# Second attention accumulator summed on VectorE, first scores in slots of their own, half-width bank last, and one gate/up tile moved from the filler to the seven-product stage

## The chip, the cores and the metric

One core of a Trainium2 chip runs the whole program. Its engines are TensorE (PE in the profile, with its weight loads as PEld), VectorE (DVE), ScalarE (ACT), GpSimd (POOL) and SyncE (SP), which here issues DMAs. Each engine works through its own instructions in order and waits on semaphores for the others. The metric is the device time of one execution in microseconds, taken as the median of several runs. The kernel before has a median of 1060.9 us in 3 runs (1057.14 to 1061.3).

## The reference

One transformer block with a parallel sum: attention and a gated MLP both read the same normalised input, and both results are added to x.

```python
xn  = layernorm(x)                                   # 2048 tokens x 640
q, k, v = split(xn @ wqkv)                           # 32 heads of 20
p   = softmax(mask(q @ k.T / sqrt(20)))              # query i sees keys i-255 .. i
att = (p @ v) @ wo
mlp = (gelu_tanh(xn @ w_gate) * (xn @ w_up)) @ w_down   # inner width 1728
out = x + att + mlp
```

All of it is float32; the mask is a sliding window of 256 keys.

## The kernel before, in words

**Products in three passes.** A float32 product is computed as three products of split operands (high x high, low x high, high x low), each of five 128-row steps, so one 128x512 result of `xn @ w` is 15 matmuls (`dense_steps`, L105 in the profile). Where two gate/up results are wanted for two token chunks at once, `gate_up_pair` (matmuls at L935) computes them with seven block products in place of eight: 54 matmuls for each pair of chunks, 108 for a gate/up tile over all 2048 tokens, where the plain way takes 120.

**Stages.** (1) Layer norm, transposes and the first q/k and v projections, up to about 92 us. (2) Attention, in 32 units, about 92 to 627 us. A unit is 4 heads by one chunk of 512 queries. (3) The pairs: the half tile `rest[0]` plain and then gate/up tiles 6 to 12 by `gate_up_pair`, to about 812 us. (4) The down and output projections, also by seven products (L1202), to the end.

**A unit of attention.** It has 14 slots (`NS`). Each slot emits a few instructions of attention and then pulls matmuls from a generator, `filler()`, at a mean of `RATE / NS` a slot: the remaining q/k/v projections and gate/up tiles 0 to 5. The list `sets` says in which order the filler takes them. Before slot 0 of the first unit a ramp pulls some 112 filler matmuls. The instructions of PE, ACT, DVE and POOL are emitted in exactly this order; SP's order is set by a scheduler.

- *Maxima.* `max_pair` makes two 128x320 score tiles on PE (`ps_m`, L480) in four PSUM buffers, and DVE reduces each to row maxima (`junk`, `mx`, L490). A unit has eight pairs: two at the head of slot 0, two after the values, two each in slots 5 and 9. They run ahead of the unit that needs them.
- *Scores.* `exp_piece` makes one of 12 score pieces on PE (`ps_e`, L545) and ACT exponentiates it (L547) into a probability tile `P`. Four pieces (one for each head) fill one bank; a unit has three banks, called X, Z and Y in `pieces`, in three `P` buffers. Z is half as wide in the first chunk. `ps_e` has two PSUM buffers, tag `ex`.
- *Clearing.* One slot after a bank's fourth piece, `clear` zeroes the masked corners on POOL (L558, L561), 128x512 elements each.
- *Values.* In slot 0 of the next unit `av_unit` multiplies the banks with v (`ps_o`, L586) into two accumulators `os[0]` and `os[1]`, one for each half of the keys' rows. They take the two `ex` buffers, so the next unit's first score piece needs `os[0]` read out, and the second needs `os[1]` read out. ACT copies `os[0]` to `ob` (L592) and `os[1]` to a spare part of Y's `P` tile (L593); three slots later POOL adds the two (L596), and five slots later SP stores `ob`.

**Loads.** `load_stack` brings the stacked q and k tiles of unit u+3 (`qs`, `ks`, six DMAs each): k in slot 9 (`KSLOT`), q in slot 12. Their buffers are free when the score pieces that read the old tiles are done.

**Deferred work.** `defer(n, ...)` runs a step n slots later, `late` puts it behind the slot's attention instructions.

Of the kernel before, what the change touches and what calls it, by code (L numbers as in the profile page):

```python
# [19 lines left out]
C = 512  # L20
# [10 lines left out]
NS = 14  # L31
RATE = 42.2
V1_SLOT = 158
MXD = 7
KSLOT = 9
LAG = 3, 5, 4, 4, 4, 4, 3, 3, 4, 3, 2, 1, 1, 1
NFA = 6
HD = D // 2
# [27 lines left out]
def block_kernel(ctx, tc, x, wqk, wv, wgu, wdo, wdl, out):  # L66
# [464 lines left out]
    def exp_piece(u, s):  # L531
# [15 lines left out]
        nc.scalar.activation(pt[:, j, lo:hi], ps[:, lo:hi], AF.Exp, scale=SCALE)  # L547
        if j == 3:
            defer(1, clear, u, bi)

    def clear(u, bi):
        c = u % NC
        pt = pts[u, bi]
        for p in pieces(c)[bi]:
            for col, diag in diag_tail(*p, c):
                a = pt[:, :, col:col + 128]
                if diag:
                    nc.gpsimd.affine_select(out=a, in_=a, pattern=[[0, 4], [1, 128]], compare_op=OP.is_ge,  # L558
                                            fill=0.0, base=0, channel_multiplier=-1)
                else:  # L560
                    nc.gpsimd.affine_select(out=a, in_=a, pattern=[[0, 4], [-1, 128]], compare_op=OP.is_ge,  # L561
                                            fill=0.0, base=-1, channel_multiplier=1)

    def av_unit(u):
# [5 lines left out]
        def half(d, r):  # L570
            i = 2 * d + r
            return d, r, max(0, 64 * i), min(C, 64 * i + 320)

        steps_ = [((0, 0), (0, 1)), ((2, 0), (-1, 1)), ((-1, 0), (2, 1)), ((1, 0), (1, 1)),
                  ((3, 0), (-2, 1)), ((-2, 0), (3, 1))]
        todo = [half(*x) for pair in steps_ for x in pair if x[0] in place]
        begun_, left = set(), [sum(t[1] == r for t in todo) for r in range(2)]
        for d, r, qa, qb in todo:
# [10 lines left out]
            begun_.add(r)  # L589
        ob, oc = ap.tile([128, C], F32, name="ob", tag="ob", bufs=1), pts[u, 2][:, 0]  # L590
        lo = 0 if c else 64
        nc.scalar.activation(ob, os[0], AF.Copy)  # L592
        nc.scalar.activation(oc[:, lo:], os[1][:, lo:], AF.Copy)  # L593

        def join():
            nc.gpsimd.tensor_tensor(out=ob[:, lo:], in0=ob[:, lo:], in1=oc[:, lo:], op=OP.add)  # L596

# [4 lines left out]

        defer(3, join)
        defer(5, store)

# [183 lines left out]
    def attention():  # L789
# [696 lines left out]
```

## Time and profile before

| what | value |
|---|---|
| median of 3 runs | 1060.9 us |
| the profiled execution's own time | 1059.57 us |
| its span | 1057.7 us |
| PE busy | 1042.1 us (99%) |
| DVE, ACT, POOL busy | 722.2, 532.1, 376.0 us |
| granted TensorE clock | 0.998 on average |
| attention, `ps_o` first to last | 106.1 to 627.1 us |
| pairs, `ps_g` | 627.6 to 812.8 us |

Busy times on PE are modelled ends of pipelined matmuls: a 128x512 matmul is shown as about 0.39 us long although the next one starts about 0.23 us after it. So "99% busy" hides short waits, and they are read from starts, from weight loads that were held up, and from who released them. DMA traffic (44.7% of the DMA engines' span on SP's queue) is not what sets the pace in attention.

### The profile page before, as it was taken

To read this page: it belongs to the slowest core of one execution; us is meant where nothing else is said; L and a number is where in the kernel's file an instruction comes from. 1 tells how busy PE (TensorE), PEld (TensorE's weight loads), DVE (VectorE), ACT (ScalarE), POOL (GpSimd) and SP (SyncE) were. 2 spreads that over 40 slices of the span, in tenths; PEclk is the share of its full clock that TensorE was granted. 3 is DMA by queue.
4 is the path that set the end of the run, shared out by engine and by line. 5 is a ranking of instruction groups with operands and counts; after the bars stand their busy time and mean duration, and the time that the engine had idled before them with its cause. 6 is when DMAs were issued, how large, how long until landed. Compare 5 with 4: busy or idle time off the path is not lost.

```text
span 1057.7 us, 25616 instructions
## 1 busy us (share of the span) xinstructions
PE 1042.1 (99%) x9429; PEld 837.7 (79%) x9429; DVE 722.2 (68%) x1985; ACT 532.1 (50%) x1120; POOL 376.0 (36%) x550
## 2 busy tenths in 40 slices
PE   8999999999999999999999999999999999999998
PEld 7977666666678766676666778888888999999998
DVE  7745656565554566766666537787775869888887
ACT  4434665566756566565665665223324544333332
POOL 6021765778664484647556451111100000000000
PEclk9999999999999999999999999999999999999999
DMA  5552353546453253434334125576667774443333
GB/s 204 186 157 71 106 175 109 149 122 191 128 159 94 77 167 102 148 100 138 106 111 128 41 82 198 185 252 235 232 234 265 257 235 128 127 138 110 122 128 105
DMA packets 105190, 158.74 MB, mean 150 GB/s; under 512 B 15420, under 2 KB 60092, under 8 KB 105064
## 3 DMA queue, kind: packets, MB, share of 16 engines
q1 hardware_dynamic: 102680, 150.95, 44.7%
q10 hardware_dynamic: 2384, 6.16, 1.8%
q8 instruction: 74, 1.21, 0.5%
q14 instruction: 52, 0.43, 0.1%
HBM read 101.78 MB, written 54.92 MB: 148 GB/s over the span
## 4 chain that ended last, share of the span: by engine, by line
PE 82%; DVE 6%; POOL 4%; issue 3%; DMA 3%; ACT 2%; SPq 1%; ACTq 0%; DVEq 0%; POOLq 0%
PE ps_d L105 24%; PE ps L1202 17%; PE ps_g L935 16%; PE ps_e L545 7%; PE ps_v L105 6%; PE ps_o L586 5%; PE ps_m L480 4%; POOL pt L247 1%; PE ps_g L105 1%; DVE junk L490 1%; DVE ss L1040 1%; POOL P L561 1%; POOL P L558 1%; DMA hr<-hd 1%; DMA stg<-wtd 1%
## 5 line engine op out<-in xcount | busy, mean ns | idle before, releaser
L490 DVE CUSTOM_DVE_ANT_0 junk<-ps_m,mask 128x320 bf16<-128x320 f32 (+2 forms) x512 | 243.1, 475 | 166.2 <-PE ps_m L480 108.4
L547 ACT ACTIVATE P<-ps_e 128x512 f32<-128x512 f32 (+2 forms) x384 | 198.7, 571 | 94.7 <-PE ps_e L545 85.4
L1202 PE MATMUL ps<-wb,at 128*128 128x320 f32 x999 | 157.1, 310 | 2.2 <-DVE at L1040 2.2
L1202 PEld LDWEIGHTS ps<-wb,at 128*128 128x128 f32 x999 | 149.6, 189 | 3.0 <-DVE at L1040 2.7
L105 PE MATMUL ps_d<-xh,wql 128*128 128x512 f32 x430 | 131.4, 415 | 0.0
L105 PE MATMUL ps_d<-xl,wqh 128*128 128x512 f32 x430 | 130.2, 412 | 0.0
L105 PE MATMUL ps_d<-xh,wqh 128*128 128x512 f32 x430 | 130.0, 413 | 0.0
L558 POOL TENSOR_SCALAR_AFFINE_SELECT P<-P 128x512 f32<-128x512 f32 x128 | 83.5, 653 | 102.7 <-ACT P L547 100.3
L545 PE MATMUL ps_e<-qs,ks 124*128 124x128 bf16 (+2 forms) x704 | 117.7, 278 | 0.7 <-ACT P L547 0.4
L105 PEld LDWEIGHTS ps_d<-xl,wqh 128*128 128x128 f32 x430 | 78.7, 189 | 15.0 <-issue 1.6
L105 PEld LDWEIGHTS ps_d<-xh,wql 128*128 128x128 f32 x430 | 78.4, 189 | 14.6 <-issue 1.2
L1202 PE MATMUL ps<-wt,at 128*128 128x320 f32 x552 | 90.0, 312 | 0.0
L105 PEld LDWEIGHTS ps_d<-xh,wqh 128*128 128x128 f32 x430 | 78.2, 189 | 14.6 <-issue 1.1
L545 PEld LDWEIGHTS <-ks 124*128 124x128 bf16 x704 | 49.6, 98 | 50.3 <-issue 36.7
L1202 PEld LDWEIGHTS ps<-wt,at 128*128 128x128 f32 x552 | 83.8, 189 | 0.2
L561 POOL TENSOR_SCALAR_AFFINE_SELECT P<-P 128x512 f32<-128x512 f32 x112 | 71.2, 646 | 27.8 <-ACT P L547 27.8
L1156 ACT ACTIVATE at<-ss 128x512 fp32r<-128x512 f32 x59 | 37.3, 632 | 86.5 <-DVE ss L1040 86.5
L586 PE MATMUL ps_o<-P,v 64*32 64x320 f32 (+4 forms) x2816 | 76.0, 348 | 1.1 <-POOL P L561 0.8
L247 POOL TENSOR_TENSOR pt<-r,pt 128x512 bf16<-128x512 f32 x40 | 46.6, 1166 | 76.8 <-ACT pt L246 75.3
L586 PEld LDWEIGHTS ps_o<-P,v 64*32 64x32 f32 x2816 | 48.5, 106 | 26.8 <-POOL P L561 3.6
L480 PE MATMUL ps_m<-ks,qs 60*64 60x320 bf16 (+3 forms) x1472 | 62.6, 260 | 3.0 <-DVE mx L490 1.2
L480 PEld LDWEIGHTS <-qs 60*64 60x64 bf16 x1472 | 28.2, 105 | 41.9 <-issue 37.2
(195 smaller groups left out, 1742.8 us busy)
## 6 DMA issues: line engine op xcount, KB each, us to landing
hr<-hd SPq DMA_DIRECT2D x104, 128.0 KB
hd<-he SPq DMA_DIRECT2D x50, 256.0 KB
wr<-wgu SPq DMA_DIRECT2D x27, 320.0 KB
qs<-qd SPq DMA_DIRECT2D x64, 120.0 KB
ks<-kd SPq DMA_DIRECT2D x64, 120.0 KB
xi<-x SPq DMA_DIRECT2D x16, 320.0 KB
qs<-qd SPq DMA_DIRECT2D x64, 80.0 KB
ks<-kd SPq DMA_DIRECT2D x64, 80.0 KB
```

The source lines that it names most:

```text
L105: nc.tensor.matmul(ps, a(k), b(k), start=n == 0, stop=n == 3 * nk - 1)
L247: nc.gpsimd.tensor_tensor(out=pt[:, l, :], in0=r, in1=pt[:, 1, :], op=OP.subtract)
L480: nc.tensor.matmul(ps[64 * h:64 * h + 64, col:col + w], q[rows, j, q0:q0 + 64], ks_, start=True, stop=True, tile_position=(64 * r, 64 * h))
L490: nc.vector.tensor_tensor_reduce(out=junk[:, 0:n], in0=ps[:, 320 - n:320], in1=mask[:, 320 - n:320], scale=1.0, scalar=NEG, op0=OP.add, op ...
L545: nc.tensor.matmul(ps[:, col:col + n], k[0:QROWS, j, kc:kc + 128], q[0:QROWS, j, q0:q0 + n], start=True, stop=True)
L547: nc.scalar.activation(pt[:, j, lo:hi], ps[:, lo:hi], AF.Exp, scale=SCALE)
L558: nc.gpsimd.affine_select(out=a, in_=a, pattern=[[0, 4], [1, 128]], compare_op=OP.is_ge, fill=0.0, base=0, channel_multiplier=-1)
L561: nc.gpsimd.affine_select(out=a, in_=a, pattern=[[0, 4], [-1, 128]], compare_op=OP.is_ge, fill=0.0, base=-1, channel_multiplier=1)
L586: nc.tensor.matmul(os[r][32 * j:32 * j + 32, qa:qb], v[rows, w0_:w0_ + 32], pt[rows, j, col + qa - q0:col + qb - q0], start=r not in begun ...
L935: nc.tensor.matmul(ps, i, j, start=first and n == 0, stop=n == len(work) - 1, skip_group_check=True)
L1156: nc.scalar.activation(hi[:, 3:7], s, AF.Copy)
L1202: nc.tensor.matmul(ps[bank][:, 0:HD], *work[bank][j], start=bank not in begun, stop=final[p, bank] == n and j == len(work[bank]) - 1, skip ...
```

## The change

Five things are changed together.

1. `os[1]` is no longer copied by ACT and added by POOL. One DVE instruction adds it from PSUM to `ob` (`join`). It stands after the third maximum pair of slot 0 and ahead of the fourth. The store follows three slots after slot 0 in place of five.
2. The first two score pieces stand in slots 1 and 2, one each (`EXPS`), with a whole slot's filler between them; before, both stood in slot 1 with one filler matmul between. The other ten stay in pairs in slots 3 to 11.
3. The banks come in the order X, Y, Z, and Z's clearing is done in two halves, two heads each, after its second and its fourth piece. The values take Z last.
4. q and k of unit u+3 are both loaded from slot 12.
5. Gate/up tile 5 leaves the filler (`NFA` 6 to 5) and becomes one more tile of the pairs. `RATE` falls from 42.2 to 38.8, the second v projection starts at slot 169 in place of 158, and `sets` takes q/k tiles 2 and 3 ahead of gate/up tile 0.

```diff
-RATE = 42.2
-V1_SLOT = 158
+RATE = 38.8
+V1_SLOT = 169
-KSLOT = 9
+KSLOT = 12
+EXPS = {1: (0,), 2: (1,), 3: (2, 3), 5: (4, 5), 7: (6, 7), 9: (8, 9), 11: (10, 11)}
-NFA = 6
+NFA = 5
...
-        return X, Z, Y
+        return X, Y, Z
...
-        if j == 3:
-            defer(1, clear, u, bi)
+        if bi == 2 and j % 2:
+            defer(1, clear, u, bi, slice(j - 1, j + 1))
+        elif j == 3:
+            defer(1, clear, u, bi, slice(0, 4))
...
-        steps_ = [((0, 0), (0, 1)), ((2, 0), (-1, 1)), ((-1, 0), (2, 1)), ((1, 0), (1, 1)),
-                  ((3, 0), (-2, 1)), ((-2, 0), (3, 1))]
+        steps_ = [((0, 0), (0, 1)), ((1, 0), (1, 1)), ((3, 0), (-2, 1)), ((-2, 0), (3, 1)),
+                  ((2, 0), (-1, 1)), ((-1, 0), (2, 1))]
...
         nc.scalar.activation(ob, os[0], AF.Copy)
-        nc.scalar.activation(oc[:, lo:], os[1][:, lo:], AF.Copy)
 
         def join():
-            nc.gpsimd.tensor_tensor(out=ob[:, lo:], in0=ob[:, lo:], in1=oc[:, lo:], op=OP.add)
+            lo = 0 if c else 64
+            nc.vector.tensor_tensor(out=ob[:, lo:], in0=os[1][:, lo:], in1=ob[:, lo:], op=OP.add)
...
-        defer(3, join)
-        defer(5, store)
+        defer(3, store)
+        return join
...
-    sets = [("qk", 1), ("gu", 0), ("qk", 2), ("qk", 3), ("qk", 4)]
+    sets = [("qk", 1), ("qk", 2), ("qk", 3), ("gu", 0), ("qk", 4)]
...
                 if i == 0 and u:
-                    av_unit(u - 1)
+                    join = av_unit(u - 1)
                     flush()
-                    pull_max(2, T)
-                if i % 2 and i < 12 and u < NU:
-                    exp_piece(u, i - 1)
-                    if i == 1 and u:
-                        pull_fill(1)
-                        debt[0] -= 1
-                    exp_piece(u, i)
+                    pull_max(1, T)
+                    join()
+                    pull_max(1, T)
+                if u < NU:
+                    for s in EXPS.get(i, ()):
+                        exp_piece(u, s)
                 flush()
-                if u + 3 < NU and i in (KSLOT, 12):
-                    load_stack(u + 3, (int(i == KSLOT),))
+                if u + 3 < NU and i == KSLOT:
+                    load_stack(u + 3)
```

The changed kernel issues 8009 matmuls in place of 8021 (`ps_d` 1290 to 1170, `ps_g` 816 to 924, all others alike).

How the instructions stand on DVE in slot 0 after the values of the 22nd unit. Each pair has two reduces (`junk`), each followed by the read of its accumulator (`mx`). Before:

```order
L490 ISA junk_7944,mx_7715<-ps_m_7938,mask_156 128x320
L490 ISA mx_7715 128x1
L490 ISA junk_7944,mx_7715<-ps_m_7939,mask_156 128x320
L490 ISA mx_7715 128x1
L490 ISA junk_7953,mx_7715<-ps_m_7947,mask_156 128x320
L490 ISA mx_7715 128x1
L490 ISA junk_7953,mx_7715<-ps_m_7948,mask_156 128x320
L490 ISA mx_7715 128x1
L499 TENSOR_SCALAR nm1_190<-mx_7715 128x16
```

And in the changed kernel, the same place:

```order
L491 ISA junk_7851,mx_7626<-ps_m_7845,mask_156 128x320
L491 ISA mx_7626 128x1
L491 ISA junk_7851,mx_7626<-ps_m_7846,mask_156 128x320
L491 ISA mx_7626 128x1
L598 TENSOR_TENSOR ob_7843<-ps_o_7794,ob_7843 128x512
L491 ISA junk_7861,mx_7626<-ps_m_7855,mask_156 128x320
L491 ISA mx_7626 128x1
L491 ISA junk_7861,mx_7626<-ps_m_7856,mask_156 128x320
L491 ISA mx_7626 128x1
L500 TENSOR_SCALAR nm1_190<-mx_7626 128x16
```

The sum of the second accumulator (`ps_o_7794`) now stands behind the two reduces of the third pair and ahead of the two of the fourth.

On PE, from the filler that follows those pairs to the second score piece (`ps_e`, two matmuls a piece). Before:

```order
L105 MATMUL ps_d_7823<-xl1_81,wqh_7287 128x512 x3
L545 LDWEIGHTS ks1_186
L545 MATMUL ps_e_7962<-qs1_183,ks1_186 128x128
L545 LDWEIGHTS ks2_187
L545 MATMUL ps_e_7962<-qs1_183,ks2_187 128x384
L105 MATMUL ps_d_7968<-xh2_78,wqh_7125 128x512
L545 LDWEIGHTS ks1_186
L545 MATMUL ps_e_7970<-qs1_183,ks1_186 128x128
L545 LDWEIGHTS ks2_187
L545 MATMUL ps_e_7970<-qs1_183,ks2_187 128x384
L105 MATMUL ps_d_7968<-xh2_78,wqh_7125 128x512 x4
```

In the changed kernel:

```order
L106 MATMUL ps_d_7722<-xl3_83,wqh_6589 128x512 x3
L546 LDWEIGHTS ks1_186
L546 MATMUL ps_e_7871<-qs1_183,ks1_186 128x128
L546 LDWEIGHTS ks2_187
L546 MATMUL ps_e_7871<-qs1_183,ks2_187 128x384
L106 MATMUL ps_d_7875<-xh3_79,wqh_6829 128x512 x3
L546 LDWEIGHTS ks1_186
L546 MATMUL ps_e_7883<-qs1_183,ks1_186 128x128
L546 LDWEIGHTS ks2_187
L546 MATMUL ps_e_7883<-qs1_183,ks2_187 128x384
L106 MATMUL ps_d_7875<-xh3_79,wqh_6829 128x512 x2
```

Between the first piece and the second stand three filler matmuls in place of one.

The end of attention on PE, from the last filler matmuls that attention has. Before:

```order
L545 MATMUL ps_e<-qs_183,ks_188 128x384
L105 MATMUL ps_d<-xh_79,wql 128x512 x5
L105 MATMUL ps_d<-xl_83,wqh 128x512 x4
L586 MATMUL ps_o<-P,v 32x320 x8
L586 MATMUL ps_o<-P,v 32x256 x8
L586 MATMUL ps_o<-P,v 32x192 x8
L586 MATMUL ps_o<-P,v 32x320 x8
L586 MATMUL ps_o<-P,v 32x128 x8
L586 MATMUL ps_o<-P,v 32x64 x8
L105 MATMUL ps_d<-xl_83,wqh 128x512
L105 MATMUL ps_g<-xh_77,wqh 128x512 x5
```

In the changed kernel:

```order
L106 MATMUL ps_d<-xl_83,wqh 128x512 x4
L546 LDWEIGHTS ks_187
L546 MATMUL ps_e<-qs_183,ks_187 128x256
L546 LDWEIGHTS ks_188
L546 MATMUL ps_e<-qs_183,ks_188 128x256
L546 LDWEIGHTS ks_187
L546 MATMUL ps_e<-qs_183,ks_187 128x256
L546 LDWEIGHTS ks_188
L546 MATMUL ps_e<-qs_183,ks_188 128x256
L589 MATMUL ps_o<-P,v 32x320 x16
L589 MATMUL ps_o<-P,v 32x128 x8
```

The filler now ends ahead of the last two score pieces, and the last values follow those pieces directly.

More of the change, by code (lines that the diff above doesn't have):

```diff
@@ L547, in exp_piece, with clear @@
         nc.scalar.activation(pt[:, j, lo:hi], ps[:, lo:hi], AF.Exp, scale=SCALE)
-        if j == 3:
-            defer(1, clear, u, bi)
-    def clear(u, bi):
+        if bi == 2 and j % 2:
+            defer(1, clear, u, bi, slice(j - 1, j + 1))
+        elif j == 3:
+            defer(1, clear, u, bi, slice(0, 4))
+    def clear(u, bi, js):
         c = u % NC
@@ L555, in clear @@
             for col, diag in diag_tail(*p, c):
-                a = pt[:, :, col:col + 128]
+                a, n = pt[:, js, col:col + 128], js.stop - js.start
                 if diag:
-                    nc.gpsimd.affine_select(out=a, in_=a, pattern=[[0, 4], [1, 128]], compare_op=OP.is_ge,
+                    nc.gpsimd.affine_select(out=a, in_=a, pattern=[[0, n], [1, 128]], compare_op=OP.is_ge,
                                             fill=0.0, base=0, channel_multiplier=-1)
                 else:
-                    nc.gpsimd.affine_select(out=a, in_=a, pattern=[[0, 4], [-1, 128]], compare_op=OP.is_ge,
+                    nc.gpsimd.affine_select(out=a, in_=a, pattern=[[0, n], [-1, 128]], compare_op=OP.is_ge,
                                             fill=0.0, base=-1, channel_multiplier=1)
```

3 lines of the change are left out of this document (1 added, 2 removed).

## The prediction

> **What bounds the kernel now.** First the page: the busy shares and the chain of work that ended last.
>
> ```profile
> PE 1042.1 (99%) x9429; PEld 837.7 (79%) x9429; DVE 722.2 (68%) x1985; ACT 532.1 (50%) x1120; POOL 376.0 (36%) x550
> ...
> PE 82%; DVE 6%; POOL 4%; issue 3%; DMA 3%; ACT 2%; SPq 1%; ACTq 0%; DVEq 0%; POOLq 0%
> ```
>
> PE sets the pace. No other engine is near its limit, so the others matter only where PE waits for one of them. Two things follow: taking matmuls away gains their full price, and a new wait of PE costs its full length. Next, stretches of time (columns: length, then busy us of PE, PEld, DVE, ACT, POOL, granted clock, DMA share, GB/s): one gate/up tile of the seven-product stage, a normal unit of attention, and two units in which POOL is crowded.
>
> ```profile
> 654.00:678.50 24.50, 24.50 (x110) 20.29 (x109) 18.91 (x30) 9.10 (x17) 3.72 (x3) 1.00 0.47 152
> 460.70:477.30 16.60, 16.60 (x208) 11.51 (x204) 11.32 (x39) 10.35 (x20) 8.37 (x15) 1.00 0.34 102
> 225.60:259.60 34.00, 33.45 (x387) 21.99 (x387) 20.29 (x73) 22.31 (x47) 27.40 (x38) 1.00 0.59 170
> ```
>
> PE is full in the tile and in the normal unit. In the crowded units POOL is busy 27.40 of 34.00 us, and they last 17.0 us each in place of 16.6.
>
> Third, slot 0 to the second score piece of a normal unit in order of time (start, length, engine, line, what):
>
> ```profile
> 460.66 2.45 PE L586 MATMUL ps_o<-P,v 64*32 64x320 f32 x96
> ...
> 463.04 0.47 PE L480 MATMUL ps_m<-ks,qs 60*64 60x320 bf16 x8
> 463.12 0.60 ACT L592 ACTIVATE ob<-ps_o 128x512 f32<-128x512 f32 x1 [3.26 <-PE ps_o L586]
> 463.42 0.49 DVE L490 CUSTOM_DVE_ANT_0 junk<-ps_m,mask 128x320 bf16<-128x320 f32 x1 [0.34 <-PE ps_m L480]
> ...
> 463.44 0.96 PE L105 MATMUL ps_d<-xl,wqh 128*128 128x512 f32 x3
> 463.61 0.60 ACT L593 ACTIVATE P<-ps_o 128x512 f32<-128x512 f32 x1
> ...
> 464.06 0.49 DVE L490 CUSTOM_DVE_ANT_0 junk<-ps_m,mask 128x320 bf16<-128x320 f32 x1
> ...
> 464.24 0.39 PE L545 MATMUL ps_e<-qs,ks 124*128 124x128 bf16 x2
> 464.29 1.29 POOL L596 TENSOR_TENSOR ob<-ob,P 128x512 f32<-128x512 f32 x1 [3.00 <-ACT P L593]
> ...
> 464.34 0.53 PE L105 MATMUL ps_d<-xh,wqh 128*128 128x512 f32 x1
> ...
> 464.70 0.49 DVE L490 CUSTOM_DVE_ANT_0 junk<-ps_m,mask 128x320 bf16<-128x320 f32 x1
> ...
> 464.71 0.40 PE L545 MATMUL ps_e<-qs,ks 124*128 124x128 bf16 x2
> ```
>
> ACT has both accumulators out of PSUM by 464.21. The second score piece, which takes the second accumulator's buffer, starts at 464.71, half a microsecond later, so PE doesn't wait. DVE gets the third pair at 463.42, since PE makes that pair only behind the values, and is at the reduces of the third and fourth pair, 0.64 us apiece from start to start, until 466.0.
>
> **The change, part by part.**
>
> *The tile that moves.* The filler loses 120 matmuls of 128x512, the pairs gain 108 of the same shape. The first of the three rows above is one gate/up tile: two calls of 54 matmuls (of the 110 counted, two were in flight at the edges), 24.50 / 108 = 0.227 us each. At that price attention gets 27.2 us shorter and the pairs 24.5 us longer: -2.7 us. The new tile's elementwise work is covered by the pairs' full PE (DVE 18.91 of 24.50 us); without that cover it would cost what exceeds the PE time, which is nothing here.
>
> *The sum of the second accumulator.* These groups price what goes and, as the nearest row, what comes:
>
> ```profile
> L596 POOL TENSOR_TENSOR ob<-ob,P 128x512 f32<-128x512 f32 (+1 forms) x32 | 40.1, 1252 | 44.2 <-ACT P L593 44.2
> ...
> L593 ACT ACTIVATE P<-ps_o 128x512 f32<-128x512 f32 (+1 forms) x32 | 18.6, 581 | 0.0
> ...
> L261 DVE TENSOR_TENSOR r<-ps_d,pt 128x512 f32<-128x512 f32 x40 | 27.5, 689 | 42.1 <-ACT pt L265 29.3 <-POOL pt L247 12.8
> ```
>
> POOL loses 40.1 us and ACT 18.6 us; DVE gains 32 x 0.69 = 22.1 us (a sum of one PSUM and one SBUF operand, as in L261). None of these is PE time. But the sum now frees the buffer of the second score piece, and it stands behind the third pair's reduces, which cannot start before PE has made that pair. In the unit above it would start where the fourth pair's first reduce starts now, 464.70, end at 465.39, and release PE at 465.44 (about 0.05 us from release to start, by the rows further down). Two more filler matmuls between the pieces bring PE there at 464.71 + 2 x 0.227 = 465.16. PE waits 0.28 us. Behind the sum on DVE the fourth pair's reduces are 0.69 us later; PE asks for their buffers in slot 5, over 3 us later, so I put nothing on it. A unit ahead of a first chunk, whose pieces are single matmuls:
>
> ```profile
> 497.73 0.34 PE L545 MATMUL ps_e<-qs,ks 124*128 124x384 bf16 x1
> ...
> 498.15 0.34 PE L545 MATMUL ps_e<-qs,ks 124*128 124x384 bf16 x1
> ...
> 498.37 0.49 DVE L490 CUSTOM_DVE_ANT_0 junk<-ps_m,mask 128x320 bf16<-128x320 f32 x1
> ```
>
> Here the order has two filler matmuls ahead of the first piece and three between (before, three and one), so the second comes at 498.15 + 0.23 = 498.38, while the sum is released at 498.37 + 0.74 = 499.11: 0.73 us. The same subtraction, with each unit's own filler counts, for the 29 units that still have maxima behind the values gives 0 in three units, 0.76 us at most, and 10.7 us together, 0.37 us a unit. Bounds: 0, if PE comes later everywhere, and 29 x 0.76 = 22.0 us. I take 10.7, as it is read unit by unit.
>
> *POOL relieved, half-width bank last.* Where POOL is late, the values wait in the middle:
>
> ```profile
> 243.25 0.63 POOL L561 TENSOR_SCALAR_AFFINE_SELECT P<-P 128x512 f32<-128x512 f32 x1
> ...
> 243.92 0.19 PEld L586 LDWEIGHTS ps_o<-P,v 64*32 64x32 f32 x16 [1.01 <-POOL P L561]
> 244.51 0.18 PEld L586 LDWEIGHTS ps_o<-P,v 64*32 64x32 f32 x16 [0.40 <-POOL P L558]
> ```
>
> The waits of all units together (total us, times, longest):
>
> ```profile
> PEld ps_o L586 <- POOL P L561: 3.6, 7, 1.0
> PEld ps_o L586 <- POOL P L558: 3.4, 9, 0.4
> ```
>
> The clear in the first fence ends at 243.88 and PE goes on 0.04 us later. In all, 7.0 us of weight loads were held for clearing. Clearing only half tiles last, of a bank that the values take last, without 1.25 us of summing ahead of them on POOL, gives the clears more than 1 us of room in each unit, so most of this goes. But loads run ahead of running matmuls: of the 7.0 us, PE itself lost less. I take -3 us, bounds 0 (POOL stays late because the q/k tiles, whose splits are POOL work, come earlier) and -7. The 56 more clears, 112 of them half-size, lie in POOL's idle time.
>
> *Scores apart, shorter units.* Each exponential of the second piece now starts later, and in four units the order puts 0.6 to 1.2 us of other ACT work between the first two, which can hold the fourth piece. Every slot also has 2.77 filler matmuls in place of 3.01, 0.05 us less cover. No row prices it; bounds 0 and +5 us (32 units by 0.15 us), taken +2.
>
> *q and k from slot 12.* SP's rows of one unit's q loads:
>
> ```profile
> 473.22 1.02 SPq L455 DMA_DIRECT2D qs<-qd  x3
> ...
> 475.03 1.02 SPq L455 DMA_DIRECT2D qs<-qd  x3
> ```
>
> The twelve issues take some 4.1 us of SP's time at that pace. k comes 2 us later than now and q as now; the first pair that reads either stands in slot 5 of the next unit, over 8 us behind slot 11's last score. What queues behind them on SP is stores that nobody waits for. Cost: nothing; were that room gone, up to 2 us a unit.
>
> *The end of attention.*
>
> ```profile
> 622.26 0.61 PE L545 MATMUL ps_e<-qs,ks 124*128 124x128 bf16 x4
> ...
> 622.57 1.46 PE L105 MATMUL ps_d<-xh,wql 128*128 128x512 f32 x5
> 622.83 1.12 ACT L547 ACTIVATE P<-ps_e 128x512 f32<-128x512 f32 x2
> ...
> 623.87 1.07 PE L105 MATMUL ps_d<-xl,wqh 128*128 128x512 f32 x4
> ...
> 624.87 2.45 PE L586 MATMUL ps_o<-P,v 64*32 64x320 f32 x96
> ```
>
> Nine filler matmuls cover the last two exponentials, which end at 623.95. Changed, no filler is left there; the values need both score buffers, so they start about when those exponentials end, 1.0 to 1.2 us after PE is ready. I take +1.0, bounds 0 and, with the last half clear (0.63 us for two heads at most) and a slower clock (next), 3.3.
>
> ```profile
> 863.05 1.00 PE L1202 MATMUL ps<-wb,at 128*128 128x320 f32 x5 [1.87 <-DVE at L1040]
> ```
>
> ```profile
> 860.00:870.00 10.00, 8.13 (x46) 7.87 (x45) 8.95 (x19) 3.92 (x9) 0.00 (x0) 0.83 0.59 198
> ```
>
> After a wait of 1.87 us the granted clock averages 0.83 over 10 us: 1.7 us of clock lost. The wait at the end of attention is shorter, so I put no such loss in the sum and 1.7 us in its upper bound.
> The Trainium skill ("TensorE: Matmul & The Clock Gate", What's actually happening) says that the gate halves the clock after an idle window of some 3.4 us. By that rule a wait of 1 us at the end of attention would cost only itself and the sum would stay as it is; by the row, if 1 us were enough as 1.87 us was, it would be 1.7 us more. The row differs from a reading of the rule in which PE must be idle for a whole window.
>
> **The sum.** -2.7 + 10.7 - 3 + 2 + 1 = +8.0 us against the profiled execution's 1059.6 us: 1067.6 us. That execution lies 1.3 us under the median of the runs, 1060.9, and inside their 1057.1 to 1061.3, so I leave the number as it is: 0.6% over the median. About 0.5%, 5.3 us, is what a measurement of this kernel tells from no change; the bounds are 1055.6 and 1066.2.
>
> **The rivals.** (a) *The sum stays hidden* and the kernel gets faster. Place: the second score piece of each unit. Price: 10.7 us falls away, which leaves 1056.9 us, and 1053 with all of POOL's 7 us. It decides where PE's mean wait there is under 2.7 / 29 = 0.09 us. For it: PE comes late anyway in every fourth unit, where it waits for DVE's earlier reduces. Against it: both rows above are short by 0.28 and 0.73 us. (b) *The wait is half as long*, because PE comes later by waits that I don't see: 5 us less, 1062 us. (c) *DVE becomes the bound of slot 0 to 5*: the 0.69 us is handed on through the fourth pair to slot 5, as the filler's own DVE work (0.69 us and more an instruction) falls into the same stretch. Another 0.3 us in each of 29 units is 9 us: 1077 us. Against it: DVE is busy 11.32 of 16.60 us. (d) *The relief is nothing* since the crowded units have other POOL work: 3 us more, 1071 us, inside my own case's range.
>
> **How the numbers follow.** My case, with (d), has 0.57: 1062 to 1073, three quarters of it over 1066.2. (a) has 0.18, spread about 1056, two thirds of it under 1055.6. (b) 0.13: no change. (c) 0.12: slower. Slower: 0.57 x 0.75 + 0.12 = 0.55; faster: 0.18 x 2/3 = 0.12; the same: 0.33. The range leaves out the lower half of (a) and the end of (c): 1055 to 1075.
>
> **What would show it.** Right: in slot 2 of nearly each unit the second score piece waits for DVE's sum, 0.2 to 0.8 us; the waits of weight loads for clears are mostly gone; attention ends 13 to 20 us earlier and not 27, the pairs last 24.5 us longer at a full PE. Wrong: second pieces that start within 0.1 us of their filler's end, or PE waits in slots 5 and 9 for DVE larger than in slot 2, or a gap over 2 us where attention ends.

## The result, and the profile after

The changed kernel takes 1069.7 us (median; 1069.2 to 1071.1 in four runs), the kernel before 1060.4 us (1057.1 to 1061.3 in four runs) beside it. The ratio is 1.0096 with a 95% interval of 1.0075 to 1.0116: 10.2 us slower, between 8.0 and 12.3. The prediction said 1067.6 us, with "slower" as the likeliest. The profiled execution takes 1071.1 us with a span of 1069.4 us, 11.7 us more than the span before. Of the page, the busy shares and the engines of the chain that ended last:

```profile
PE 1049.8 (98%) x9417; PEld 839.6 (79%) x9417; DVE 740.6 (69%) x2028; ACT 518.0 (48%) x1088; POOL 342.8 (32%) x566
...
PE 79%; DVE 6%; DMA 4%; ACT 3%; POOL 3%; issue 2%; SPq 2%; ACTq 0%; DVEq 0%; POOLq 0%
```

POOL and ACT lost work and DVE gained some, as the change says. But PE, which has 12 matmuls less to do, is busy a smaller share of a longer span, and the chain goes more often over ACT and DMA. Where the time lies shows when the span is cut at the same places in both kernels: from the first values to those of the 13th unit, the 18 units from there, the end of attention, the pairs, the last stage (length, then busy us of PE, PEld, DVE, ACT, POOL, granted clock, DMA share, GB/s). Before:

```profile
106.12:310.35 204.23, 201.91 (x2418) 137.39 (x2414) 123.86 (x445) 128.53 (x268) 143.23 (x214) 1.00 0.49 143
310.35:609.87 299.52, 298.33 (x3604) 210.75 (x3600) 183.46 (x656) 181.30 (x396) 169.87 (x259) 1.00 0.36 110
609.87:627.58 17.71, 17.71 (x260) 12.75 (x260) 2.77 (x4) 11.13 (x22) 9.84 (x14) 1.00 0.23 75
627.58:812.62 185.04, 185.04 (x817) 153.15 (x816) 138.63 (x228) 64.01 (x116) 20.61 (x14) 1.00 0.64 219
812.62:1054.32 241.70, 239.51 (x1616) 238.30 (x1614) 205.02 (x442) 100.35 (x179) 0.00 (x0) 0.99 0.49 157
```

After:

```profile
108.02:310.97 202.95, 197.26 (x2369) 130.92 (x2365) 125.12 (x455) 119.80 (x245) 128.87 (x222) 0.99 0.47 142
310.97:601.25 290.28, 287.73 (x3549) 199.66 (x3546) 187.21 (x666) 171.41 (x378) 152.12 (x266) 1.00 0.36 111
601.25:617.07 15.82, 15.20 (x247) 10.60 (x246) 4.26 (x6) 9.61 (x19) 8.04 (x12) 1.00 0.17 55
617.07:826.70 209.63, 209.63 (x928) 173.52 (x925) 150.82 (x251) 70.73 (x129) 20.89 (x14) 1.00 0.59 203
826.70:1065.57 238.87, 237.94 (x1616) 236.76 (x1614) 204.19 (x440) 99.94 (x179) 0.00 (x0) 1.00 0.49 158
```

The pairs are 24.6 us longer at a full PE. A unit has 3.4 filler matmuls less, 0.77 us. The 18 later units should then be 13.9 us shorter and are 9.2 us shorter: 4.7 us of new time. The 12 early units should be 9.3 us shorter and are 1.3 us shorter: 8.0 us of new time. So the loss has two places: a little in most later units, and a lot in a few early ones. (The first values come 1.9 us later and the last stage is 2.8 us shorter; the last section shows what goes with both, and why neither is put down to the change.)

Every unit first. Slot 0 to the second score piece of a later unit, PE, DVE and ACT in order of time:

```profile
473.51 2.55 PE L589 MATMUL ps_o<-P,v 64*32 64x320 f32 x96
...
475.99 0.47 PE L481 MATMUL ps_m<-ks,qs 60*64 60x320 bf16 x8
476.03 0.60 ACT L594 ACTIVATE ob<-ps_o 128x512 f32<-128x512 f32 x1 [2.68 <-PE ps_o L589]
...
477.01 0.49 DVE L491 CUSTOM_DVE_ANT_0 junk<-ps_m,mask 128x320 bf16<-128x320 f32 x1
477.19 0.39 PE L546 MATMUL ps_e<-qs,ks 124*128 124x128 bf16 x2
...
477.43 0.08 DVE L491 DVE_READ_ACCUMULATOR2_ANT mx<- 128x1 f32 x1
477.43 0.68 DVE L598 TENSOR_TENSOR ob<-ps_o,ob 128x512 f32<-128x512 f32 x1
...
478.03 0.48 DVE L491 CUSTOM_DVE_ANT_0 junk<-ps_m,mask 128x320 bf16<-128x320 f32 x1
...
478.17 0.23 PE L546 MATMUL ps_e<-qs,ks 124*128 124x128 bf16 x1
```

The sum stands behind the third pair's second reduce, as the prediction has it, but starts 0.42 us after that reduce and not 0.64 us. It ends at 478.11 and the second piece starts at 478.17. With the first piece at 477.19 and three filler matmuls between, PE would have been there at about 477.19 + 0.23 + 3 x 0.227 = 478.10: a wait of 0.07 us. From the values to the first pair it is 2.48 us here; in the unit that the prediction shows of before it is 2.38 us (463.04 less 460.66).

The early units: in the sixth, the values wait in the middle (POOL and PE in order of time), and a row of two stretches follows, ahead of that wait and from it on (the columns as above):

```profile
194.80 1.16 POOL L248 TENSOR_TENSOR pt<-r,pt 128x512 bf16<-128x512 f32 x1
195.91 0.41 POOL L564 TENSOR_SCALAR_AFFINE_SELECT P<-P 128x256 f32<-128x256 f32 x1
196.27 0.41 POOL L561 TENSOR_SCALAR_AFFINE_SELECT P<-P 128x256 f32<-128x256 f32 x1
...
196.73 1.57 PE L589 MATMUL ps_o<-P,v 64*32 64x256 f32 x28 [1.77 <-POOL P L561]
```

```profile
190.00:196.00 6.00, 4.96 (x97) 3.21 (x96) 3.18 (x11) 2.25 (x5) 6.00 (x10) 1.00 0.54 159
...
196.00:206.00 10.00, 9.27 (x80) 5.61 (x80) 5.18 (x19) 4.58 (x9) 5.00 (x9) 0.83 0.50 142
```

POOL has no pause in the six microseconds ahead. The last two half clears stand behind a 1.16 us step of a q or k row, and the values wait 1.77 us for them. Then the granted clock is 0.83 over 10 us, which is another 1.7 us. The waits of weight loads over the whole kernel (total us, times, longest), which before had 3.6 and 3.4 us for clears, none for the sum and none of the pairs' for k:

```profile
PEld ps_o L589 <- POOL P L561: 7.3, 8, 2.2
PEld L546 <- DVE ob L598: 6.6, 17, 0.8
...
PEld L481 <- DMA ks<-kd: 2.1, 5, 0.7
```

The waits for clears didn't go, and two kinds are new. Loads run ahead of running matmuls, so PE itself loses less than these sums; its own waits for clears are 3.6 us in three places, and were 0.8 us in two.

### The profile page after: what moved, and what is told of

Its sections match the earlier page's. It is cut to its first block, busy times and chain, and to the rows that moved or that the text cites. A ratio compares the mean times of both kernels' runs of the same rounds, so it can differ in the third digit from the quotient of the medians.

```text
span 1069.4 us, 25655 instructions
## 1 busy us (share of the span) xinstructions
PE 1049.8 (98%) x9417; PEld 839.6 (79%) x9417; DVE 740.6 (69%) x2028; ACT 518.0 (48%) x1088; POOL 342.8 (32%) x566
## 4 chain that ended last, share of the span: by engine, by line
PE 79%; DVE 6%; DMA 4%; ACT 3%; POOL 3%; issue 2%; SPq 2%; ACTq 0%; DVEq 0%; POOLq 0%
PE ps_d L106 20%; PE ps_g L936 18%; PE ps L1203 17%; PE ps_e L546 7%; PE ps_v L106 6%; PE ps_o L589 5%; PE ps_m L481 4%; ACT P L548 1%; DVE junk L491 1%; PE ps_g L106 1%; DMA ks<-kd 1%; POOL pt L248 1%; SPq L456 1%; DVE ss L1041 1%; POOL P L564 1%
## 5 line engine op out<-in xcount | busy, mean ns | idle before, releaser
L548 ACT ACTIVATE P<-ps_e 128x512 f32<-128x512 f32 (+2 forms) x384 | 201.6, 570 | 101.2 <-PE ps_e L546 96.1
L561 POOL TENSOR_SCALAR_AFFINE_SELECT P<-P 128x512 f32<-128x512 f32 (+1 forms) x160 | 89.0, 557 | 165.5 <-ACT P L548 165.4
L106 PE MATMUL ps_d<-xl,wqh 128*128 128x512 f32 x390 | 120.7, 417 | 0.0
L106 PE MATMUL ps_d<-xh,wqh 128*128 128x512 f32 x390 | 119.9, 415 | 0.0
L106 PE MATMUL ps_d<-xh,wql 128*128 128x512 f32 x390 | 119.8, 415 | 0.0
L589 PE MATMUL ps_o<-P,v 64*32 64x320 f32 (+4 forms) x2816 | 80.7, 351 | 4.1 <-POOL P L561 3.6
L106 PEld LDWEIGHTS ps_d<-xl,wqh 128*128 128x128 f32 x390 | 71.2, 190 | 13.5 <-issue 2.2
L106 PEld LDWEIGHTS ps_d<-xh,wql 128*128 128x128 f32 x390 | 70.8, 189 | 13.3 <-issue 1.9
L106 PEld LDWEIGHTS ps_d<-xh,wqh 128*128 128x128 f32 x390 | 70.5, 189 | 12.8 <-issue 2.1
L564 POOL TENSOR_SCALAR_AFFINE_SELECT P<-P 128x512 f32<-128x512 f32 (+1 forms) x136 | 77.0, 575 | 9.4 <-ACT P L548 9.3
L99 POOL TENSOR_TENSOR wql<-wr,wqh 128x640 fp32r<-128x640 f32 x10 | 16.1, 1610 | 155.5 <-PE ps_g L936 128.0
```

Source lines behind the costliest of these rows:

```text
L106: nc.tensor.matmul(ps, a(k), b(k), start=n == 0, stop=n == 3 * nk - 1)
L561: nc.gpsimd.affine_select(out=a, in_=a, pattern=[[0, n], [1, 128]], compare_op=OP.is_ge, fill=0.0, base=0, channel_multiplier=-1)
L564: nc.gpsimd.affine_select(out=a, in_=a, pattern=[[0, n], [-1, 128]], compare_op=OP.is_ge, fill=0.0, base=-1, channel_multiplier=1)
L589: nc.tensor.matmul(os[r][32 * j:32 * j + 32, qa:qb], v[rows, w0_:w0_ + 32], pt[rows, j, col + qa - q0:col + qb - q0], start=r not in begun ...
```

## The experiments

Each run is compared with the kernel before on the same chip; microseconds are worked out from the ratio on 1060 us. "Later units" are the 18 of the second row above, "early units" the 12 of the first. Theory A is the prediction's: the wait for the sum in every unit is the main cost. Theory B is read from the profile above: that wait is small, and the rest is the early units, the values' order and the later scores.

**e1: the sum ahead of the third pair.**

```diff
                     flush()
-                    pull_max(1, T)
                     join()
-                    pull_max(1, T)
+                    pull_max(2, T)
```

> The changed kernel with the sum of the second accumulator written directly behind the values, ahead of the third pair of maxima, so that on VectorE it stands ahead of that pair's reduces and not behind them. Theory A (the prediction): the second score piece waits for the sum, 10.7 us over all units. Then about 10 us come back and the time is 1059 to 1061 us. Theory B (read from the trace of the changed kernel): that wait is only about 2 us in all, since the sum starts 0.41 us and not 0.64 us behind the start of the reduce ahead of it. Then 0 to 2 us come back, 1067 to 1070 us, and the waits for the third pair's reduces may take even that.

Measured: 1069.9 us, ratio 1.0097 [1.0078, 1.0116]; no difference from the changed kernel. In the profile no wait for the sum is left. The same stretches, early and later units:

```profile
108.51:310.95 202.44, 196.57 (x2369) 130.87 (x2366) 125.95 (x455) 119.73 (x245) 128.76 (x222) 0.99 0.47 142
310.95:598.75 287.80, 286.15 (x3550) 199.13 (x3546) 189.57 (x666) 171.42 (x378) 152.33 (x266) 1.00 0.37 112
```

The later units are 2.5 us shorter than in the changed kernel and the early ones 0.5. So the place of the sum is worth some 3 us in the trace and not 10. The times put it at 0 with some 2.8 us either way, so 3 us stand at the edge of what they allow. The starts of the second pieces say the same: in e1 each comes as soon as its last filler matmul lets it, and in the changed kernel they come later by 4.0 us in all, by 0.1 us or less in 19 of 31 units and by 0.49 us at most. Theory A falls in its size.

**e2: the first gate/up tile early again. e3: the moved tile alone. e4: all but the tile.** e2 takes one line of the change back:

```diff
-    sets = [("qk", 1), ("qk", 2), ("qk", 3), ("gu", 0), ("qk", 4)]
+    sets = [("qk", 1), ("gu", 0), ("qk", 2), ("qk", 3), ("qk", 4)]
```

e3 makes this part on the kernel before, and e4 takes it back on e2:

```diff
-RATE = 42.2
-V1_SLOT = 158
-NFA = 6
+RATE = 38.8
+V1_SLOT = 169
+NFA = 5
```

> The changed kernel with the filler's tiles in the order of the kernel before (first q/k pair, first gate/up tile, then the other q/k pairs); all else as changed. Theory B: the changed kernel's long waits in its units 1 to 7 (values held for clears by GpSimd, k loads that land late, 6 to 9 us in all) come from the q/k pairs being first, whose splits load GpSimd and whose stores and loads crowd the queues. Then the time is 1060 to 1064 us. Theory A: the cost is in the sum, in every unit; the order of tiles is worth under 2 us: 1067 to 1070 us.

> The kernel before with one part of the change alone: one gate/up tile leaves the filler for the seven products (with the filler rate and the slot of the second v tile that go with it). Theory A: it is worth -2.7 us and at most 1 us at the end of attention: 1057 to 1059 us. Theory C: shorter units uncover waits that 25 us more of filler covered in the kernel before (0.85 us less per unit), so that the tile itself costs 2 to 6 us: 1062 to 1066 us.

> The changed kernel without the moved tile: six gate/up tiles in the filler, the filler's rate, the slot of the second v tile and the order of tiles as before; the sum on VectorE, the bank order, the split scores and the k loads as changed. Theory A: +10.7 for the sum, -3 for GpSimd, +2 for the scores: 1069 to 1071 us. Theory B: 2 us for the sum, 2.4 us for values that take 0.10 us longer in the new order, and 1 to 2 us for the split scores, less some GpSimd relief: 1062 to 1066 us. Together with the kernel before, the tile alone and the run above it gives all four combinations of the tile with the rest: if the effects add up, the run above should be this one's gain or loss plus the tile's.

Measured: e2 1066.7 us, ratio 1.0068 [1.0048, 1.0088]; e3 1058.5 us, 0.9986 [0.9972, 0.9999]; e4 1063.7 us, 1.0050 [1.0029, 1.0072]. Early and later units of e2, and of e3 with its end of attention:

```profile
105.46:304.54 199.08, 195.61 (x2370) 130.05 (x2366) 124.75 (x455) 120.31 (x245) 128.56 (x219) 1.00 0.47 137
304.54:594.80 290.26, 287.73 (x3550) 199.65 (x3546) 187.13 (x666) 171.38 (x378) 153.70 (x269) 1.00 0.38 115
```

```profile
108.23:302.80 194.57, 191.13 (x2370) 128.98 (x2366) 121.17 (x443) 125.47 (x257) 141.54 (x212) 1.00 0.49 141
302.80:588.58 285.78, 284.39 (x3550) 199.60 (x3546) 177.98 (x648) 177.96 (x396) 169.70 (x254) 1.00 0.39 117
588.58:604.88 16.30, 15.40 (x246) 10.06 (x245) 6.72 (x10) 9.97 (x19) 9.88 (x13) 1.00 0.21 64
```

With the tile alone the later units are 13.74 us shorter than before, which is the price of their filler, 13.9 us: shorter units uncover nothing there. Theory C falls: the tile gains 1.5 us [0.1, 3.0]. It does bring waits for clears, 4.0 us of PE itself in e3 where the kernel before has 0.8, but the early units still get 9.7 us shorter, as much as their filler is worth. So the changed kernel's 3.6 us of such waits are there with the tile alone, and the rest of the change doesn't take them away. All else costs 5.3 us without the tile (e4) and, with it, e2 less e3 = 8.7 us; the intervals (5.3 is 3.1 to 7.6, 8.7 is about 6.2 to 11.3) allow equal effects, the traces speak for a larger one beside the tile: the early units gain 6.5 us from e4 to e2 (205.62 to 199.08) where they gain 9.7 in e3. The order of tiles is worth 3.0 us in time, with an interval of 3 us either way; in the trace it is 3.9 us, all of it in the early units, and the later units are equal to 0.02 us. In e2 the sixth unit's long wait and its slow clock are not there (1.00 in the first row). So theory B has the place right by the trace; its size is half of what it forecast, as 7 us of waits for clears remain in e2. The time alone, 1066.7 us, lies between the two forecasts and can't decide.

**e5: the short steps of the values last.**

```diff
-        steps_ = [((0, 0), (0, 1)), ((1, 0), (1, 1)), ((3, 0), (-2, 1)), ((-2, 0), (3, 1)),
-                  ((2, 0), (-1, 1)), ((-1, 0), (2, 1))]
+        steps_ = [((0, 0), (0, 1)), ((1, 0), (1, 1)), ((2, 0), (-1, 1)), ((-1, 0), (2, 1)),
+                  ((3, 0), (-2, 1)), ((-2, 0), (3, 1))]
```

> The changed kernel with the steps of the values in another order: the two steps of the half-width bank ahead of the two short ones (128 and 64 columns), which stand last again, as in the kernel before. Theory D: the values take 2.48 us in place of 2.38 us in 24 units only because the steps that end them are the long ones (256 and 192 columns) and not the short ones. Then the values take 2.38 us again in units where GpSimd is not late, and the time falls by about 2 us, less what crowded units lose because the bank that is cleared last is read 0.2 us sooner: 1066 to 1069 us. Theory E: the 0.10 us comes from what stands behind or ahead of the values (the clears, the copy), not from the order of steps: 2.48 us stays, 1068 to 1071 us.

Measured: 1072.7 us, ratio 1.0118 [1.0101, 1.0135], 2.3 us over the changed kernel with 2.8 us either way. The values of a later unit, and early and later units:

```profile
473.92 2.45 PE L589 MATMUL ps_o<-P,v 64*32 64x320 f32 x96
...
476.30 0.47 PE L481 MATMUL ps_m<-ks,qs 60*64 60x320 bf16 x8
```

```profile
105.35:311.58 206.23, 197.30 (x2370) 132.27 (x2366) 124.09 (x455) 119.84 (x245) 128.80 (x222) 0.99 0.47 139
311.58:601.20 289.62, 286.48 (x3549) 200.68 (x3545) 186.97 (x666) 171.40 (x378) 152.07 (x266) 1.00 0.37 111
```

The values take 2.38 us again, so the 0.10 us comes from the order of the steps, and the later units are 0.7 us shorter: one of them, whose values wait for a late clear, is 0.43 us longer, and the others together 1.1 us shorter. But the early units are 3.3 us longer: the bank that is cleared last is read sooner, and where POOL is late the values last 0.3 to 0.8 us longer (4.42, 4.20 and 6.20 us in the second, third and sixth unit, against 4.07, 3.82 and 5.40). The pairs' matmuls then wait for k for 2.5 us, against 0.7. Theory D is right on the 0.10 us and wrong on the time: by these rows the new order's long steps at the end hid part of the late clears.

**e6: the first two scores paired again.**

```diff
-EXPS = {1: (0,), 2: (1,), 3: (2, 3), 5: (4, 5), 7: (6, 7), 9: (8, 9), 11: (10, 11)}
+EXPS = {1: (0, 1), 3: (2, 3), 5: (4, 5), 7: (6, 7), 9: (8, 9), 11: (10, 11)}
...
                     for s in EXPS.get(i, ()):
+                        if s == 1 and u:
+                            pull_fill(1)
+                            debt[0] -= 1
                         exp_piece(u, s)
```

> The changed kernel with the second score piece back in slot 1, one filler matmul behind the first, as in the kernel before; the sum stays on VectorE between the third and the fourth pair. If the sum is what frees the second piece's buffer, as both theories have it, that piece now waits from 1.6 us behind the end of the values to 2.1 us: 0.5 us in each of 24 units and 0.2 to 0.7 us in the seven others, 12 to 16 us of waits for the sum in all in place of 2. Theory A and B then both give 1077 to 1083 us, since the filler between the pieces does not go away but comes later. Rival: the wait is made good in slot 2, as the first copy and the reduces are then no longer on the way, and the scores' exponentials follow each other more closely: 1069 to 1073 us.

Measured: 1080.6 us, ratio 1.0204 [1.0187, 1.0221], 11.4 us slower than the changed kernel. Its waits for the sum:

```profile
PEld L546 <- DVE ob L598: 13.0, 19, 1.2
...
PE ps_e L546 <- DVE ob L598: 5.6, 15, 0.8
```

This is the wait that the prediction feared, with only one filler matmul between the pieces: PE itself now stands 15 times for the sum, 5.6 us in all in place of 0.5, and its waits for exponentials grow from 1.1 to 4.8 us. The time is as both theories say, and the rival (made good later) falls. In the trace attention is 8.1 us longer, and the last stage, which no edit touches, 2.6 us. So the sum does free the second piece's buffer, and the split of the scores is what covers it.

**e7: the sums of x spread, on the changed kernel. e8: the same with the tile alone.** These are 80 operations of 0.73 us on POOL, which prepare the seven products.

```diff
             for j, fn in enumerate(x_sums(p, k, half)):
-                at(XS0 + XSN * i + 2 * j, fn)
+                at(NS * (3 + (10 * i + j) // 3) + (1, 5, 9)[(10 * i + j) % 3], fn)
```

> The changed kernel with the 80 GpSimd operations that prepare the seven products' sums of x spread out, three in a unit from unit 3 on (slots 1, 5 and 9), where they stood in eight groups of ten at every second slot. Theory B: in units 1, 2 and 5 the last clears stand behind such operations and others on a GpSimd that has no pause, so that without them the clears come 1 to 2 us earlier. The waits of PE for clears, about 6 us, fall to 2 or 3 us: 1065 to 1068 us. Rival: the splits of the q/k pairs alone keep GpSimd late in those units: 1068 to 1071 us.

> The kernel before with the moved tile alone and the same spreading of the sums of x. If GpSimd's clears are what the shorter units wait for (about 8 us of PE in the run with the tile alone), most of that goes: 1052 to 1056 us, faster than both kernels. Rival: GpSimd is late there for the q/k and v splits: 1056 to 1059 us.

Measured: e7 1069.9 us, ratio 1.0095 [1.0067, 1.0123], no difference; e8 1055.4 us, ratio 0.9959 [0.9943, 0.9975]. In e7 the early units are 2.3 us shorter (200.63 against 202.95) and the weight loads' waits for clears fall from 7.3 to 4.7 us, of which the times show nothing: theory B's cause is there, and part of the lateness is not these operations. In e8 the early units are 1.8 us shorter than in e3 (192.80 against 194.57). By the times e8 is 2.9 us faster than e3, with 2.2 us either way. So the spread helps the kernel with the tile alone; on the changed kernel its help is seen in the trace only.

**e9: the sum alone (with the tile). e10: the banks alone (with the tile). e11: k loaded in slot 9.** e9 is e3 with the changed `av_unit` tail, join between the pairs and `EXPS`; e10 is e2 with those three as before. Both e10 and e11 have

```diff
-KSLOT = 12
+KSLOT = 9
...
-                if u + 3 < NU and i == KSLOT:
-                    load_stack(u + 3)
+                if u + 3 < NU and i in (KSLOT, 12):
+                    load_stack(u + 3, (int(i == KSLOT),))
```

> The kernel before with the moved tile, the sum on VectorE between the third and fourth pair, and the first two scores apart; banks, clears, values, k loads and the order of tiles as before. To be held against the run with the tile alone (ratio 0.9986). Theory A: +10.7 us for the wait of the second piece and +2 for the scores, less some relief of GpSimd: 1066 to 1071 us. Theory B (from the traces so far): the second piece waits 2 us for the sum, the later exponentials hold score pieces for another 3 to 4 us, and GpSimd without its 1.25 us of summing a unit gives 1 to 3 us back: 1060 to 1064 us.

> The kernel before with the moved tile and the banks' part of the change: half-width bank last, its clears in halves, the new order of the values' steps; the sum on GpSimd, paired first scores, k loads and order of tiles as before. Against the run with the tile alone. Theory A: fewer waits of the values for clears, -1 to -3 us: 1055 to 1058 us. Theory B: the values take 0.10 us longer in 24 units (2.4 us) and the early units' clears come no sooner, as four clears of half tiles (0.41 us each) take longer than three of whole ones (0.63 us) leave: 1059 to 1063 us.

> The changed kernel with the loads of k in slot 9 again and of q in slot 12. Theory A: k from slot 12 costs nothing: 1069 to 1071 us. Theory B: the pairs' waits for k (1.3 us of PE in units 3 and 6, by the trace of the changed kernel) go: 1067 to 1069 us; nothing changes behind unit 8.

Measured: e9 1063.4 us, ratio 1.0034 [1.0016, 1.0051]; e10 1076.8 us, 1.0165 [1.0134, 1.0197]; e11 1088.2 us, 1.0262 [1.0233, 1.0291].

e9 against e3: 5.1 us, with some 2.3 us either way. Its early and later units, and its waits for clears behind those of e3:

```profile
105.51:302.23 196.72, 192.73 (x2369) 128.98 (x2365) 124.54 (x455) 120.50 (x245) 127.00 (x200) 1.00 0.48 140
302.23:591.64 289.41, 286.28 (x3549) 199.82 (x3545) 186.16 (x666) 171.45 (x378) 147.61 (x236) 1.00 0.39 115
```

```profile
PEld ps_o L586 <- POOL P L561: 7.2, 8, 1.3
...
PEld ps_o L586 <- POOL P L558: 3.4, 8, 0.6
```

```profile
PEld ps_o L587 <- POOL P L562: 6.9, 8, 1.3
...
PEld ps_o L587 <- POOL P L559: 3.4, 9, 0.4
```

POOL has 40 us less to do and the values wait as long for its clears: 10.3 us against 10.6. So taking the sum from POOL relieves nothing that PE waits for. Theory B is right on the time; its 1 to 3 us of relief is not there. From e9 to e2, which adds the banks, the halved clears and the later loads, the time grows by 3.6 us (some 2.8 either way), in the traces by 2.4 us early and 0.9 us later.

e10 and e11 don't tell their terms, because a part of their output is computed from other data. There are four buffers of k, so the k of unit u + 3 goes where that of unit u - 1 is. The half-width bank reads that older k in every chunk but a group's first. Before, it was the second bank and done in slot 7. Now it is the last, read in slots 9 and 11, and a load issued in slot 9 replaces k ahead of the last two pieces, which wait for it to land. e11's waits, and its early units:

```profile
PE ps_e L546 <- DMA ks<-kd: 14.2, 4, 4.4
...
PEld L481 <- DMA ks<-kd: 0.4, 1, 0.4
```

```profile
108.57:329.40 220.83, 202.31 (x2369) 134.23 (x2365) 124.03 (x455) 119.99 (x245) 129.16 (x221) 0.96 0.45 130
```

The pairs' waits for k go, as theory B said, but 14.2 us of waits of the scores take their place, and the clock falls. What the two runs do show is that the later k load is no free choice: it comes with the bank order. The banks' part without that load can't be had in this layout, and wasn't tried with a fifth buffer.

**e12: the tile, the spread, and clears ahead of other work in their slot,** on e8:

```diff
-        return sorted(todo, key=lambda y: y[0] is max_end)
+        return sorted(todo, key=lambda y: (y[0] is max_end) - (y[0] is clear))
```

> The kernel before with the moved tile, the sums of x spread out, and within a slot the clears issued ahead of other work on GpSimd. In the run without the last edit (ratio 0.9959) PE still lost about 6 us to clears, most of them behind the 1.17 us third piece of a q or k row in the same slot. If that is the cause, 2 to 4 us go: 1051 to 1054 us. Rival: GpSimd then waits for the exponentials with the other work behind it, and later clears are late in turn: 1055 to 1058 us.

Measured: 1055.0 us, ratio 0.9952 [0.9938, 0.9966]: 5.1 us faster than the kernel before, faster than both. Its waits for clears and its early units:

```profile
PEld ps_o L586 <- POOL P L561: 1.7, 3, 0.7
...
PEld ps_o L586 <- POOL P L558: 1.4, 3, 0.6
```

```profile
108.60:299.95 191.35, 190.80 (x2369) 130.15 (x2365) 120.81 (x443) 125.64 (x257) 138.27 (x208) 1.00 0.49 143
```

The waits for clears fall from e3's 10.6 us of weight loads to 3.1 us, with POOL's work no smaller. The early units are 3.2 us shorter than in e3 and 1.4 us shorter than in e8 (192.80). Between e8 and e12 the times show no difference; between e3 and e12 they show 3.6 us, with 2 us either way. The time is 1 us outside the forecast of 1051 to 1054 and just inside the rival's range; the waits for clears say that the cause was found, as PE itself waits 0.5 us for them, and 4.0 us in e3.

## Why the prediction came out right, and what in it was wrong

The time and the sign are right: +8.0 us forecast, +10.2 measured. The terms are not all right, and errors of both signs cancel, so that the number came this near is in part luck.

| Term | Forecast, us | By runs (ratios, on 1060 us) | By traces |
|---|---|---|---|
| tile moved, end of attention | -2.7 + 1.0 | -1.5 (e3) | pairs +24.6, attention -24.8 |
| sum on DVE, scores apart | +10.7 + 2 | +5.1 (e9 less e3) | +5.2 |
| banks, clears, later loads | -3, with POOL's relief | +3.6 (e2 less e9) | +3.3 |
| q/k pairs first | 0, the bound of the relief | +3.0 (after less e2) | +3.9 |
| sum | +8.0 | +10.2 | |

The times in the third column have 1.4 to 3 us either way, and they add up to 10.2 because each is one run less the run before it. The order of adding matters too: all but the tile costs 5.3 us without the tile and 8.7 us with it, before the order of tiles.

*The tile* is as the prediction has it: 0.227 us a matmul on both sides. The end of attention lost 13 matmuls (260 to 247 in the rows), 3.0 us of filler, and became 1.9 us shorter: it costs 1.1 us, and 1.0 was forecast. The wait there is 0.56 us ahead of the values and another 0.3 us inside them, where weight loads wait for the last exponential, and the pairs behind it run at a clock of 1.00, so the upper bound with a clock loss didn't come.

*The sum* is the term that was mis-sized: 10.7 us forecast, 3 to 4 us shown (e1 against the changed kernel, by the traces). The step that failed is "it would start where the fourth pair's first reduce starts now". That is true of a reduce, which follows the reduce ahead of it at 0.64 us; the sum follows at 0.42 us. The 0.22 us, in 29 units, are 6.4 us of the 10.7, and what is left, 4.3 us, is near the 4.0 us by which the second pieces are late. The mechanism holds: e6 shows the wait at full length, and 17 weight loads wait 0.4 us on average for the sum in the changed kernel, in the range that the prediction gave, most of it under matmuls in flight. Scores apart at +2 us fits what is left of the 5.2 us in the trace, though no run has it by itself.

*POOL's relief* is the term with the wrong sign. The step "without 1.25 us of summing ahead of them on POOL" fails: the sum on POOL stood in slot 3, and ahead of the last clears, in slot 12, stand q or k rows, weight splits and sums of x (the POOL rows above). Rival (d) was true (e9). And clearing by halves isn't free: a half takes 0.41 us and a whole 0.63 us. The new order of the values' steps adds 0.10 us in each of 24 units, 2.4 us if nothing hides it; the prediction put no price on that order (e5).

*k from slot 12* was priced at nothing, and by e2 that holds with the old order of tiles, where the pairs' loads wait 0.4 us for k in all; with the q/k pairs first there are waits, in the changed kernel 2.1 us of weight loads. What the prediction missed is that this load can't stay in slot 9.

*The q/k pairs first* stood in the prediction only as a reason for which the relief might be nothing. They make it less than nothing: 3.9 us in the early units' trace, of which the sixth unit is 3.5: its wait and the clock behind it.

Rival (a), a hidden sum, would have needed a mean wait under 0.09 us a unit; 3 to 4 us over 29 units are 0.10 to 0.14, so its mechanism came near, and its time did not come because the other terms went the other way. (b) halves the wait, to 5.7 us, and so comes nearer to its size, for another reason; its time didn't come. (c) falls: PE's waits for the reduces of pairs are 1.5 us in five places, against 1.2 us in four before. Of what was to show it: the pairs came as said; attention is 12.4 us shorter and not 13 to 20; the waits for clears are not gone. And one of the prediction's own signs of being wrong came: in 19 of 31 units the second piece starts within 0.1 us of its filler's end.

## What to carry to other kernels

Price a wait by the spacing measured for that kind of neighbour in the queue: 0.2 us a step, in 29 units, was most of the largest term. Work taken from an engine helps a wait only if it stood ahead of what is waited for; read what lies directly ahead of the late instruction, and move that (against e3, e12 gained 3.6 us by an order of issue, and e9's 40 us less of POOL work shortened no wait for clears). And when the order in which buffers are read changes, look for the load that follows the last reader: it moves too.

## What the runs showed of the hardware that was not expected

- On DVE the sum behind a 128x320 reduce with an accumulator starts 0.42 us after that reduce starts, together with the read of the accumulator (477.01 and 477.43 in the rows above); a further reduce comes 0.64 us after it. The reduce behind the sum starts 0.60 us after the sum's start (478.03), while the sum's record lasts 0.68 us.
- The values' 96 matmuls hold up what follows by 2.48 us when steps of 256 and 192 columns end them, and by 2.38 us when steps of 128 and 64 do.
- A wait of PE of 1.77 us was followed by a granted clock of 0.83 over 10 us, the same loss of 1.7 us as behind the 1.87 us wait that the prediction shows; waits of 0.56 us (end of attention) and 1.03 us (second unit, at 127.4 us) had none. The length alone doesn't decide it: in e6 the values of the sixth unit wait 1.75 us for the same clears, and the granted clock is 1.00 over the next 10 us. So the 1.7 us of clock in the changed kernel's profile is no sure price of such a wait. The Trainium skill ("TensorE: Matmul & The Clock Gate", What's actually happening) has the clock halved after an idle window of some 3.4 us. The half clock over 3.4 us is what these rows add up to, but the waits ahead of it are little over half a window.
- The first values come at 105.4 to 108.6 us in the profiled executions, and the granted clock of the first stage goes with it. In the six executions in which it is 1.00 from 10 to 25 us and from 60 to 70 us (before, e2, e4, e5, e7 and e9), they come at 105.4 to 106.2 us. In the changed kernel it is 0.77 from 10 to 25 us, 3.4 us lost, and they come at 108.0 us. The edits don't sort it: e2 and e7, each a small step from the changed kernel, have the full clock there.
- The last stage is long where PE waits for DVE at its start: 242.5 us with 2.5 us of such waits in e5, 241.7 us with 2.2 us before (among them the 1.87 us that the prediction shows, with 1.7 us of clock behind them), 238.9 us with 0.3 us in the changed kernel. Why these waits differ, in a stage that no edit touches, is open. So 2 us of either stage are not read here as the effect of an edit.
